# An attention and gated-MLP kernel with a written-out order: 54 steps change places

## The chip, the cores and the metric

The kernel runs on one core of a Trainium2 chip. Times are device microseconds (us) of one launch, from the inputs in HBM to the output in HBM. The time before is 199.52 us, the median of 3 runs (199.38 to 199.70).

Five engines work beside each other: TensorE (PE in the profile, PEld for its weight loads), VectorE (DVE), ScalarE (ACT), GpSimd (POOL) and SyncE (SP), which here only issues transfers. Each engine works through its own list in order. A step that waits holds up everything behind it on its engine.

## The reference

There are two parts. Attention with a sliding window comes first, for 8 batches and 8 heads, 576 positions, 64 values a head; each position sees itself and the 63 before it. The result, 576 x 512 a batch, goes through a gated MLP whose gate mixes positions:

```python
scores = q @ k.T / 8                     # per batch and head
attn   = softmax(where(0 <= i - j < 64, scores, -1e9))
x      = attn @ v                        # heads side by side: 576 x 512
h      = relu(x @ w_in)                  # 512 -> 1024
u, v   = h[:, :512], h[:, 512:]
v_n    = (v - mean(v)) / sqrt(var(v) + 1e-6)
v_s    = w_spatial @ v_n + b_spatial     # 576 x 576, over positions
out    = (u * v_s) @ w_out               # 512 -> 512
```

Inputs and outputs are fp32; the kernel computes products in fp16 with fp32 sums.

## The kernel before

The work is cut into 1,100 or so named steps, and a text, `ORDER`, lists them all. One word is one step: name, engine, and the numbers of the buffers that it takes. `ldq2_0:DQ:0` issues on SyncE the load of q for batch 2, heads 0 to 3, into buffer 0 of its pool; `V1_3:PE:0` runs on TensorE and takes PSUM bank 0. The kernel first makes all steps with what each depends on, and then emits them in the order of the text. So the text alone decides three things: the order on every engine and on the transfer queue, which of the eight PSUM banks a product goes to, and so whose reading of that bank a product has to wait for. Nothing is rescheduled later.

In the names the first number is the batch b (0 to 7). One batch goes through these steps:

- **ldq, ldk, ldv** (DQ): loads. **cq, ck, cv** make fp16 of them, mostly on GpSimd; **tq, tk** (DVE, L416) transpose q and k; **sl, su, s4** make a copy of v that is shifted by 64 positions.
- **S** (PE, L491, L562): scores, into four banks. **E** (ACT, L500, L572): exp. **M** (DVE, L503, L576): the mask, as a minimum. **Z** (PE, L516, L585): sums over keys. **N, n** (ACT, L542, L544): one over the sum, as exp of minus log. **P** (PE, L527, L598): the product with v. **X** (DVE, L535, L606): P times one over the sum, which is x. The suffix r is the last 64 positions.
- **V0 to V4** (PE, L676, L689): the second half of x @ w_in. **Vr** (ACT, L656): relu. **Vb, Va** (DVE, L658, L660): mean and variance. **L1, L2** (ACT, L703, L705): one over the deviation, once a batch, after all five Va. **A** (DVE, L715): v_n, five steps, which all wait for L2. V4 also makes the last 64 rows of the output of the batch before (L692), and so waits for that batch's Ge4.
- **U** (PE, L731, L736) and **Ur** (ACT, L744): the first half, with relu. **G** (PE, L761, L767): w_spatial times v_n, which needs all five A. **Ge** (DVE, L775): times u. **O** (PE, L786): times w_out; it needs Ge0 to Ge3. **Oe** (ACT, L633): to SBUF. **st** (DQ): store.

W and We, cwin, cwsp, cwo are the preparation of the weights, in the first 43 us. Batches overlap: while U and G of batch b run, scores of b + 1 are made, and loads for b + 2 and later are on their way. All loads are issued by SyncE on one queue, in the order of the text.

A product needs its bank to be empty. `G0_1:PE:0` goes into bank 0, which U0_1 had filled, and waits for Ur0_1 on ScalarE to have read it. Where a step of TensorE is moved, its bank is given anew, and so it may wait for another reader than before.

Of the kernel before, what the change touches and what calls it, by code (L numbers as in the profile page):

```python
# [59 lines left out]
Ge1_4:DVE:6 M2_r:DVE cv2_0:POOL:0 cv2_2:POOL sl2_0:POOL:0 su2_2:DVE sl2_2:DVE su2_0:POOL  # L60
cq3_1:POOL:1 cq4_0:POOL:2 ck3_0:POOL:3 N2_00:ACT:4 N2_01:ACT:2 n2_01:ACT s42:ACT n2_00:ACT
Ge1_3:DVE:7 Ge1_0:DVE:8 cq3_0:POOL:0 Z2_r:PE:7 P2_10:PE:5 P2_00:PE:0 Z2_10:PE:4 P2_r:PE:2
P2_01:PE:1 N2_r:ACT:5 n2_r:ACT X2_r:DVE:0 N2_10:ACT:0 n2_10:ACT st0_0:DQ Z2_11:PE:7 N2_11:ACT:3
P2_11:PE:3 V2_4:PE:2 U2_4:PE:4 Vr2_4:ACT:3 n2_11:ACT Oe1_4:ACT:0 X2_00:DVE:0 Ge1_2:DVE:9 X2_01:DVE
X2_10:DVE:1 X2_11:DVE O1_2:PE:0 O1_3:PE:7 Oe1_2:ACT:0 Ur2_4:ACT:4 Oe1_3:ACT tq3_1:DVE:1
tk3_0:DVE:2 V2_2:PE:6 V2_3:PE:1 Vr2_3:ACT:0 tq3_0:DVE:3 S3_1:PE:5:2:3:0 Vr2_2:ACT:2 E3_110:ACT:0
E3_111:ACT V2_0:PE:4 Vr2_0:ACT:6 V2_1:PE:7 Vr2_1:ACT:4 E3_100:ACT:3 S3_0:PE:1:6:3:0 Vb2_3:DVE:3
Va2_3:DVE Vb2_2:DVE:2 M3_11:DVE Vb2_0:DVE:1 ldv3_0:DQ:1 ldv3_1:DQ Va2_2:DVE ldk4_0:DQ:0
ldv3_2:DQ:3 cv3_0:POOL:1 sl3_0:POOL:1 s43:POOL Vb2_4:DVE:4 Va2_4:DVE Va2_0:DVE ck4_0:POOL:1
Vb2_1:DVE:5 Va2_1:DVE E3_000:ACT:2 E3_101:ACT E3_001:ACT M3_00:DVE E3_010:ACT:1 L12:ACT:0 L22:ACT  # L70
st1_1:DQ st0_1:DQ ldv3_3:DQ U2_1:PE:4 U2_0:PE:7 U2_2:PE:5 M3_10:DVE A2_1:DVE:0 ldq4_1:DQ:5
A2_2:DVE:1 ldv4_0:DQ:2 Ur2_0:ACT:3 E3_011:ACT A2_0:DVE:2 Ur2_2:ACT:5 Ur2_1:ACT:1 U2_3:PE:1
O1_0:PE:2 O1_1:PE:6 S3_r:PE:3:7:0:5 Oe1_0:ACT:0 Ur2_3:ACT:2 su3_0:POOL cv3_2:POOL su3_2:POOL
E3_r0:ACT:1 E3_r1:ACT E3_r2:ACT Z3_10:PE:4 Z3_11:PE:2 Z3_00:PE:1 Oe1_1:ACT N3_10:ACT:1 ldv4_1:DQ
sl3_2:POOL cq4_1:POOL:3 ldv4_4:DQ:1 ldk4_1:DQ:4 A2_3:DVE:3 A2_4:DVE ldv4_2:DQ:0 st1_0:DQ
ldq5_0:DQ:6 ldv4_3:DQ st1_4:DQ ldk5_0:DQ:1 E3_r3:ACT N3_11:ACT:5 n3_11:ACT N3_00:ACT:4 cv4_0:ACT:0
G2_3:PE:3 G2_1:PE:7 n3_00:ACT n3_10:ACT M3_01:DVE tq4_0:DVE:4 tk4_0:DVE:5 G2_2:PE:0 G2_0:PE:6
Ge2_3:DVE:0 M3_r:DVE Ge2_1:DVE:1 Z3_r:PE:4 P3_10:PE:5 Z3_01:PE:2 P3_00:PE:1 P3_11:PE:3 N3_r:ACT:2
Ge2_2:DVE:2 P3_01:PE:7 P3_r:PE:0 Ge2_0:DVE:3 N3_01:ACT:0 n3_01:ACT ck4_1:ACT:0 X3_10:DVE:2
X3_00:DVE:3 n3_r:ACT S4_0:PE:4:6:2:5 E4_010:ACT:3 E4_000:ACT:2 X3_01:DVE X3_11:DVE E4_001:ACT  # L80
O2_0:PE:1 Oe2_0:ACT:1 E4_011:ACT G2_4:PE:7 V3_2:PE:3 V3_1:PE:2 ldv5_0:DQ:4 Vr3_2:ACT:5 Vr3_1:ACT:1
V3_0:PE:4 tk4_1:DVE:0 Ge2_4:DVE:4 tq4_1:DVE:1 X3_r:DVE:1 Vr3_0:ACT:7 S4_1:PE:6:7:1:5 ldq5_1:DQ:2
E4_100:ACT:0 E4_110:ACT:1 E4_111:ACT M4_00:DVE M4_01:DVE Z4_00:PE:3 V3_4:PE:0 Vb3_2:DVE:0
# [6 lines left out]
ldv7_4:DQ:0 ldv6_2:DQ:2 Oe2_1:ACT ldv6_3:DQ ldv5_1:DQ ldq6_0:DQ:0 st2_4:DQ Ur3_4:ACT:0 Ur3_2:ACT:2  # L90
Oe2_2:ACT:0 U3_0:PE:3 Oe2_3:ACT n4_01:ACT Ur3_1:ACT:1 cq5_1:POOL:0 su4_0:POOL U3_3:PE:2
Ur3_3:ACT:5 su4_2:POOL G3_2:PE:4 Z4_10:PE:0 Ur3_0:ACT:3 Z4_11:PE:6 Z4_r:PE:5 cq6_1:DVE:3
Ge3_2:DVE:6 sl4_2:POOL P4_10:PE:7 P4_00:PE:1 P4_01:PE:2 N4_10:ACT:4 n4_10:ACT N4_11:ACT:0
N4_r:ACT:5 n4_11:ACT ck5_1:ACT:2 P4_r:PE:3 P4_11:PE:0 X4_00:DVE:0 X4_10:DVE:1 X4_01:DVE G3_0:PE:4
G3_4:PE:1 ldv5_4:DQ:1 S5_0:PE:6:5:7:2 E5_000:ACT:0 E5_001:ACT X4_11:DVE V4_0:PE:0 V4_2:PE:6
# [769 lines left out]
```

## Time and profile before

| what | before |
|---|---|
| median of 3 runs | 199.52 us |
| profiled execution, whole | 199.67 us |
| its span, first to last instruction | 198.0 us |
| TensorE busy | 185.9 us, 94% |
| VectorE busy | 168.7 us, 85% |
| ScalarE busy | 152.3 us, 77% |
| GpSimd busy | 90.8 us, 46% |
| granted TensorE clock | 1.0 |

The page of the profile gives busy time per engine, the span in 40 slices, the chain of work that ended last, and the costliest groups of instructions. The timeline lists instructions by their start in us from the beginning of the span; neighbours of one kind are merged to one row with their count. In square brackets behind a row stands how long the engine had been idle before it, and whose work ended that.

### The profile page before, as it was taken

The numbers are of one execution on the slowest core, as the hardware profiler recorded it, in microseconds if no ns is written. First come the engines' busy times: TensorE is split into PE (matmuls) and PEld (weight loads), VectorE is DVE, ScalarE is ACT, GpSimd is POOL, SyncE is SP. The second block draws the span as 40 slices with busy tenths as digits, with TensorE's granted clock in tenths as the row PEclk, the third lists the DMA queues.
The fourth block names the chain that finished last, engine by engine and source line by source line (L and its number), as shares of the span: only waits on it lengthen the run. The fifth ranks groups of instructions, "written<-read, shape, count | busy, mean of one in ns | idle before, by whom it ended". The sixth has DMA issues, their size and how long they took to land.

```text
span 198.0 us, 7037 instructions
## 1 busy us (share of the span) xinstructions
PE 185.9 (94%) x2953; PEld 99.6 (50%) x2953; DVE 168.7 (85%) x315; ACT 152.3 (77%) x326; POOL 90.8 (46%) x161
## 2 busy tenths in 40 slices
PE   7587999999989999999999999999999999999992
PEld 5464456454435554374546544654456455544450
DVE  5989999998999999999989999987998676538530
ACT  2068699997978989998899797977899986704642
POOL 4077853629668966628937990399200000000000
PEclk9999999999999999999999999999999999999999
DMA  6999999999999999999999969565050000006345
GB/s 208 346 194 360 393 317 244 296 405 280 199 316 318 240 287 259 293 342 367 236 250 256 282 186 304 135 173 193 0 209 10 0 7 3 0 0 220 125 165 209
DMA packets 49506, 42.68 MB, mean 216 GB/s; under 512 B 38593, under 2 KB 38721, under 8 KB 49474
## 3 DMA queue, kind: packets, MB, share of 16 engines
q1 hardware_dynamic: 49250, 41.90, 70.4%
q8 instruction: 23, 0.38, 0.8%
q10 hardware_dynamic: 224, 0.33, 0.5%
q14 instruction: 9, 0.07, 0.1%
HBM read 32.79 MB, written 9.44 MB: 213 GB/s over the span
## 4 chain that ended last, share of the span: by engine, by line
PE 53%; DVE 20%; DMA 13%; SPq 7%; POOL 2%; issue 1%; ACT 0%; POOLq 0%
PE bank L761 12%; PE bank L786 11%; PE bank L731 8%; PE bank L676 7%; DMA nv<-in_v_dram 5%; DMA nk<-in_k_dram 5%; DVE st L658 4%; DMA nq<-in_q_dram 4%; SPq L432 4%; DVE qT L416 4%; DVE vn L715 3%; PE bank L527 3%; DVE e L503 3%; PE bank L491 3%; PE bank L516 2%; DVE kT L416 2%
## 5 line engine op out<-in xcount | busy, mean ns | idle before, releaser
L500 ACT ACTIVATE e<-bank 128x512 f16<-128x512 f32 x64 | 34.6, 602 | 8.9 <-PE bank L491 8.3
L761 PE MATMUL bank<-wspT,vn 128*128 128x512 f16 (+1 forms) x160 | 38.7, 380 | 1.2 <-DVE vn L715 0.9
L775 DVE TENSOR_TENSOR g<-bank,ru 128x512 f16<-128x512 f32 (+1 forms) x40 | 24.5, 625 | 12.2 <-PE bank L761 9.1
L731 PE MATMUL bank<-x,win 128*128 128x512 f16 x128 | 31.1, 379 | 0.0
L656 ACT ACTIVATE vs<-bank 128x512 f16<-128x512 f32 (+1 forms) x40 | 22.7, 601 | 10.5 <-PE bank L676 7.9
L786 PE MATMUL bank<-wout,g 128*128 128x512 f16 x128 | 30.8, 379 | 0.0
L676 PE MATMUL bank<-win,x 128*128 128x512 f16 x128 | 30.7, 379 | 0.0
L633 ACT COPY ob<-bank 128x512 f32<-128x512 f32 (+1 forms) x39 | 22.4, 592 | 9.6 <-PE bank L786 9.3
L306 POOL CAST hq<-nq 128x384 f16<-128x384 f32 x39 | 21.2, 583 | 15.2 <-DMA nq<-in_q_dram 15.2
L306 POOL CAST hv<-nv 128x512 f16<-128x512 f32 x26 | 17.7, 694 | 20.7 <-DMA nv<-in_v_dram 12.3
L658 DVE BATCH_NORM_STATS2 st<-vs 128x6 f32<-128x512 f16 (+1 forms) x40 | 25.6, 665 | 1.5 <-ACT vs L656 1.5
L503 DVE TENSOR_TENSOR e<-e,mask 128x1024 f16<-128x1024 f16 x32 | 25.7, 820 | 0.0
L306 POOL COPY hs<-hv 64x512 f16<-64x512 f16 x36 | 23.8, 685 | 3.1 <-ACT hv L298 1.8
L761 PEld LDWEIGHTS <-vn 128*128 128x128 f16 (+1 forms) x160 | 14.9, 97 | 19.6 <-DVE vn L715 2.5
L744 ACT ACTIVATE ru<-bank 128x512 f32<-128x512 f32 (+1 forms) x40 | 21.6, 570 | 2.9 <-PE bank L736 1.6
L535 DVE TENSOR_TENSOR x<-bank,lz 128x512 f16<-128x512 f32 x32 | 20.4, 676 | 2.6 <-ACT lz L544 2.5
L416 DVE STREAM_TRANSPOSE qT<-hq 128x576 f32<-128x576 f32 x16 | 19.9, 1242 | 1.0 <-POOL hq L306 0.9
L416 DVE STREAM_TRANSPOSE kT<-hk 128x576 f32<-128x576 f32 x16 | 19.8, 1239 | 0.6 <-POOL hk L306 0.6
L544 ACT ACTIVATE lz<-lz 128x512 f32<-128x512 f32 x32 | 20.0, 646 | 0.2
L542 ACT ACTIVATE lz<-bank 128x512 f32<-128x512 f32 x32 | 18.6, 621 | 1.6 <-PE bank L516 1.4
L676 PEld LDWEIGHTS <-x 128*128 128x128 f16 x128 | 11.8, 98 | 14.0 <-issue 0.4
L786 PEld LDWEIGHTS <-g 128*128 128x128 f16 x128 | 11.8, 98 | 13.8 <-DVE g L775 0.8
(85 smaller groups left out, 276.3 us busy)
## 6 DMA issues: line engine op xcount, KB each, us to landing
nq<-in_q_dram SPq DMA_DIRECT2D x16, 576.0 KB, 7.2
nk<-in_k_dram SPq DMA_DIRECT2D x16, 576.0 KB, 7.2
...
```

What stands on the lines that cost most here:

```text
L306: nc.gpsimd.tensor_copy(o[:, lo:lo + step], i[:, lo:lo + step])
L416: d = add(f"t{name}{b}_{g}", ("DVE", 1.09), key, lambda e: nc.vector.transpose(qt.t[:, :].rearrange("p (i j) -> p j i", j=18), h.t[:, :].b ...
L500: ex.append(add(f"E{b}_{g}{u}{w}", ("ACT", 0.475), key, lambda e, u=u, w=w: nc.scalar.activation(e2[u].t[:, w, :], sc[2 * u + w].t[:, :], ...
L503: mins.append(add(f"M{b}_{g}{u}", ("DVE", 0.602), key, lambda e, u=u: nc.vector.tensor_tensor(e2[u].t[:, :, :], e2[u].t[:, :, :], mask[:, ...
L633: lambda e: (nc.vector.tensor_copy if last else nc.scalar.copy)(view(), m.t[rows, 0:n]),
L656: rl = add(f"Vr{b}_{j}", ("ACT", 0.476), key, lambda e: nc.scalar.activation(vs.t[0:jn, :], m.t[0:jn, :], AF.Relu), deps=[pv], acq=[vs], u ...
L658: s1 = add(f"Vb{b}_{j}", ("DVE", 0.595), key + 0.02, lambda e: nc.vector.bn_stats(st6.t[0:jn, 0:6], vs.t[0:jn, :]), deps=[rl], acq=[st6], ...
L676: nc.tensor.matmul(m.t[:, :], xr(b, r)[:, 128 * j:128 * j + 128], w_in_sb[r][:, 512:1024], start=(r == 0), stop=(r == 3))
L731: nc.tensor.matmul(m.t[:, :], w_in_sb[r][:, 128 * i:128 * i + 128], xr(b, r), start=(r == 0), stop=(r == 3))
L761: nc.tensor.matmul(m.t[:, :], w[0:kn, 128 * i:128 * i + 128], wspT[kk][0:kn, 0:512], start=(kk == 0), stop=(kk == 4))
L775: lambda e, m=m, g=g, ru=ru, n=n: nc.vector.tensor_tensor(g.t[:, 0:n], m.t[:, 0:n], ru.t[:, 0:n], ALU.mult),
L786: nc.tensor.matmul(m.t[:, :], G[r][0].t[:, 128 * j:128 * j + 128], w_out_sb[r][:, :], start=(r == 0), stop=(r == 3))
```

## The change

The kernel's functions stay as they are; only `ORDER` differs. No step changes its engine, none is added or removed. Counted on each engine, 18 steps of TensorE, 25 of ScalarE, 9 of VectorE and two transfers stand in another place. On GpSimd the order is the same. Many PSUM banks are numbered anew; most of that is a renaming in which a product still follows the same reader.

The moves, by place (times are those of the profile before):

| place | moves |
|---|---|
| A, 29 to 43 us | cwsp0 ahead of L20; Ur0_2 ahead of N1_00; Ur0_4 behind We4; Ur0_1 ahead of n1_00; W0 ahead of W2; We3 ahead of We2; cwsp4 ahead of A0_1; G0_2 ahead of Z1_r; M1_10 ahead of sl1_1 and su1_1; Z1_10 ahead of P1_r, P1_00, P1_01; N1_10 ahead of cwo10 |
| B, 35 to 57 us | load ldk2_0 ahead of ldq2_0; V1_3 ahead of V1_0 |
| C, 57 to 85 us | G1_4 ahead of Z2_00; Z2_10 ahead of P2_10 and P2_00; M2_r behind sl2_2; Ge1_2 ahead of X2_r; O1_2 ahead of V2_4; n2_11 ahead of Vr2_4; U2_4 from behind V2_4 to behind U2_2, with Ur2_4; V2_3 ahead of V2_2; E3_100 ahead of Vr2_1; U2_0 from behind U2_1 to behind Z3_00, with Ur2_0; store st0_1 ahead of st1_1 |
| D, 85 to 106 us | E4_000 ahead of E4_010; O2_1 ahead of U3_4; Vr3_3 ahead of E4_r0; n4_00 ahead of E4_r1; Ur3_2 and Oe2_1 ahead of L13; L23, Ur3_4 and Oe2_2 ahead of E4_r3; M4_10 ahead of the five A3; tq5_0 ahead of M4_r; P4_00, P4_10, P4_01 ahead of Z4_r; n4_11 ahead of N4_r |
| E, 110 to 113 us | bank of V4_4: after V4_1 (read by Vr4_1) where it was after G3_0 (read by Ge3_0) |
| F, 113 to 121 us | U4_0 from behind Z5_r to ahead of V4_3; U4_4 from behind V4_3 to behind Z5_r, with Ur4_4; N5_00 and E5_111 ahead of Vr4_3; E5_r3 behind Vr4_3; Vb4_3 behind Va4_2, Va4_3 behind M5_r |
| G, 132 to 158 us | Vr5_0 ahead of Vr5_3; Oe4_2 ahead of E6_r3; O4_1 from behind U5_2 to behind G5_4, with Oe4_1 behind n6_01; Z6_00 behind Z6_r; U5_1 ahead of G5_4; n6_00 ahead of n6_01; E7_000 ahead of E7_010; E7_r2 ahead of Vr6_1 |

The core of the diff, for places B, D and F:

```diff
-P1_10:PE:1 X1_r:DVE:1 U1_4:PE:7 M1_11:DVE cwo10:ACT cwo11:POOL N1_10:ACT:3 cwo00:POOL ldq2_0:DQ:0
-ldk2_0:DQ:3 X1_00:DVE:2 Ge0_0:DVE:4 P1_11:PE:3 cwo01:ACT Ur1_4:ACT:5 n1_10:ACT Z1_11:PE:0
...
-ck2_0:POOL:0 tk2_0:DVE:2 cq2_0:POOL:1 O0_2:PE:7 V1_0:PE:6 V1_3:PE:0 ldk2_1:DQ:4 V1_1:PE:2
...
+ldwo0:DQ:0 P1_10:PE:3 X1_r:DVE:1 U1_4:PE:4 M1_11:DVE cwo10:ACT cwo11:POOL cwo00:POOL ldk2_0:DQ:2
+ldq2_0:DQ:3 X1_00:DVE:2 Ge0_0:DVE:4 P1_11:PE:0 cwo01:ACT Ur1_4:ACT:5 n1_10:ACT Z1_11:PE:2
...
+ck2_0:POOL:0 tk2_0:DVE:2 cq2_0:POOL:1 O0_2:PE:4 V1_3:PE:6 V1_0:PE:2 ldk2_1:DQ:4 V1_1:PE:1
...
-ldq6_1:DQ:7 E4_r0:ACT:0 Vr3_3:ACT:2 Vb3_3:DVE:1 Va3_0:DVE E4_r1:ACT E4_r2:ACT n4_00:ACT Va3_3:DVE
-L13:ACT:1 E4_r3:ACT L23:ACT U3_4:PE:0 A3_2:DVE:4 A3_4:DVE A3_0:DVE:5 M4_10:DVE cq5_0:POOL:1
...
+Vr3_3:ACT:2 E4_r0:ACT:0 Vb3_3:DVE:1 Va3_0:DVE n4_00:ACT Ur3_2:ACT:0 E4_r1:ACT E4_r2:ACT Va3_3:DVE
+O2_1:PE:5 Oe2_1:ACT U3_4:PE:6 L13:ACT:1 M4_10:DVE cq5_0:POOL:1 L23:ACT A3_2:DVE:4 A3_4:DVE
...
-Vb4_0:DVE:0 Vb4_1:DVE:4 V4_3:PE:7 Vr4_3:ACT:4 U4_4:PE:2 U4_1:PE:6 N5_00:ACT:2 Va4_4:DVE M5_10:DVE
-Vb4_3:DVE:2 Va4_0:DVE U4_2:PE:4 G3_1:PE:0 ldv5_3:DQ Ur4_4:ACT:4 E5_111:ACT Va4_3:DVE Va4_1:DVE
...
-Z5_01:PE:7 Ur4_1:ACT:2 L14:ACT:0 L24:ACT Z5_r:PE:5 U4_0:PE:2 O3_0:PE:3 Ur4_2:ACT:0 sl6_0:POOL:0
...
+cv6_0:POOL:0 sl5_0:POOL:1 U4_0:PE:1 V4_3:PE:3 Vr4_3:ACT:4 U4_1:PE:0 Vb4_3:DVE:2 U4_2:PE:7
+E5_r3:ACT M5_r:DVE G3_1:PE:4 Va4_3:DVE Ge3_1:DVE:9 Z5_10:PE:5 Z5_01:PE:6 Ur4_1:ACT:4 L14:ACT:0
+L24:ACT Z5_r:PE:3 U4_4:PE:2 Ur4_4:ACT:0 O3_0:PE:0 Ur4_2:ACT:1 sl6_0:POOL:0 cv5_2:POOL A4_2:DVE:0
```

More of the change, by code (lines that the diff above doesn't have):

```diff
@@ new lines @@
+sl1_3:POOL su1_3:POOL N1_r:ACT:2 n1_r:ACT E1_110:ACT:3 E1_111:ACT cv1_1:DVE M1_10:DVE Z1_10:PE:2
+N1_10:ACT:3 sl1_1:DVE ldwo1:DQ:1 su1_1:DVE s41:POOL P1_r:PE:7 Ge0_2:DVE:3 P1_00:PE:5 P1_01:PE:1
+ldwo0:DQ:0 P1_10:PE:3 X1_r:DVE:1 U1_4:PE:4 M1_11:DVE cwo10:ACT cwo11:POOL cwo00:POOL ldk2_0:DQ:2
+ldq2_0:DQ:3 X1_00:DVE:2 Ge0_0:DVE:4 P1_11:PE:0 cwo01:ACT Ur1_4:ACT:5 n1_10:ACT Z1_11:PE:2
+V1_4:PE:7 O0_0:PE:5 X1_01:DVE N1_11:ACT:1 n1_11:ACT X1_10:DVE:3 X1_11:DVE Oe0_4:ACT:0 ldq2_1:DQ:5
+ck2_0:POOL:0 tk2_0:DVE:2 cq2_0:POOL:1 O0_2:PE:4 V1_3:PE:6 V1_0:PE:2 ldk2_1:DQ:4 V1_1:PE:1
@@ L60 @@
[L60 to L83, printed above, removed]
@@ L90 @@
[L90 to L95, printed above, removed]
@@ L120 @@
-E6_r3:ACT s47:POOL Ur5_2:ACT:4 Oe4_2:ACT:1 Oe4_3:ACT Oe4_0:ACT:0 Z6_01:PE:0 Z6_11:PE:4 Z6_00:PE:2
-M6_r:DVE A5_0:DVE:4 P6_r:PE:6 Z6_r:PE:3 Oe4_1:ACT P6_00:PE:5 P6_10:PE:7 ck7_0:POOL:0 cq7_0:POOL:2
-A5_2:DVE:5 A5_3:DVE:6 A5_4:DVE N6_r:ACT:5 N6_11:ACT:1 Z6_10:PE:1 n6_r:ACT N6_10:ACT:2 N6_01:ACT:4
-N6_00:ACT:3 n6_10:ACT n6_01:ACT n6_00:ACT A5_1:DVE:7 G5_4:PE:3 su7_2:POOL tq7_0:DVE:2 U5_1:PE:4
-G5_1:PE:1 U5_3:PE:0 Ge5_4:DVE:5 tk7_0:DVE:3 X6_10:DVE:0 Ur5_1:ACT:2 Ur5_3:ACT:0 n6_11:ACT
-X6_00:DVE:1 X6_r:DVE:0 G5_2:PE:3 Ge5_1:DVE:6 Ge5_2:DVE:7 S7_0:PE:2:7:4:5 P6_01:PE:0 X6_01:DVE
@@ new lines @@
+cv2_0:POOL:0 cv2_2:POOL sl2_0:POOL:0 su2_2:DVE sl2_2:DVE su2_0:POOL cq3_1:POOL:1 cq4_0:POOL:2
+ck3_0:POOL:3 E2_r3:ACT N2_00:ACT:4 M2_r:DVE N2_01:ACT:2 n2_01:ACT s42:ACT n2_00:ACT Ge1_3:DVE:7
+Ge1_0:DVE:8 cq3_0:POOL:0 st0_0:DQ Ge1_2:DVE:9 Z2_r:PE:4 Z2_10:PE:7 N2_r:ACT:5 n2_r:ACT P2_10:PE:6
+P2_00:PE:1 P2_r:PE:5 P2_01:PE:3 X2_r:DVE:0 N2_10:ACT:0 n2_10:ACT Z2_11:PE:4 N2_11:ACT:3 P2_11:PE:0
+n2_11:ACT O1_2:PE:2 V2_4:PE:7 Vr2_4:ACT:3 Oe1_4:ACT:0 X2_00:DVE:0 X2_01:DVE X2_10:DVE:1 X2_11:DVE
+O1_3:PE:5 Oe1_2:ACT:0 Oe1_3:ACT tq3_1:DVE:1 tk3_0:DVE:2 V2_3:PE:1 V2_2:PE:4 Vr2_3:ACT:0
@@ new lines @@
+A2_0:DVE:2 Ur2_2:ACT:3 Ur2_1:ACT:5 U2_3:PE:1 O1_0:PE:6 O1_1:PE:4 S3_r:PE:0:5:7:3 Oe1_0:ACT:1
+Ur2_3:ACT:1 su3_0:POOL cv3_2:POOL su3_2:POOL E3_r0:ACT:1 E3_r1:ACT E3_r2:ACT Z3_10:PE:2 Z3_11:PE:6
+Z3_00:PE:1 Oe1_1:ACT N3_10:ACT:1 ldv4_1:DQ sl3_2:POOL cq4_1:POOL:3 ldv4_4:DQ:1 ldk4_1:DQ:4
+A2_3:DVE:3 A2_4:DVE ldv4_2:DQ:0 st1_0:DQ ldq5_0:DQ:6 U2_0:PE:0 Ur2_0:ACT:2 ldv4_3:DQ st1_4:DQ
+ldk5_0:DQ:1 E3_r3:ACT N3_11:ACT:5 n3_11:ACT N3_00:ACT:4 cv4_0:ACT:0 G2_3:PE:5 G2_1:PE:7 n3_00:ACT
+n3_10:ACT M3_01:DVE tq4_0:DVE:4 tk4_0:DVE:5 G2_2:PE:4 G2_0:PE:2 Ge2_3:DVE:0 M3_r:DVE Ge2_1:DVE:1
@@ new lines @@
+E5_010:ACT:3 E5_011:ACT Vr4_0:ACT:6 tq5_1:DVE:0 Vr4_1:ACT:0 Vr4_2:ACT:3 G3_3:PE:1 tk5_1:DVE:1
+M5_00:DVE Ge3_4:DVE:5 X4_r:DVE:0 Ge3_0:DVE:7 S5_r:PE:4:3:6:2 E5_r0:ACT:1 E5_r1:ACT E5_r2:ACT
+V4_4:PE:7 Z5_00:PE:5 Vr4_4:ACT:5 S5_1:PE:0:4:3:6 tq6_1:DVE:4 Ge3_3:DVE:8 E5_110:ACT:2 E5_100:ACT:1
+Oe3_4:ACT:0 E5_101:ACT M5_01:DVE Vb4_2:DVE:5 Vb4_4:DVE:3 Vb4_0:DVE:0 Vb4_1:DVE:4 N5_00:ACT:2
+Va4_4:DVE M5_10:DVE Va4_0:DVE ldv5_3:DQ E5_111:ACT Va4_1:DVE Va4_2:DVE cv5_0:POOL:1 cq6_0:POOL:1
+cv6_0:POOL:0 sl5_0:POOL:1 U4_0:PE:1 V4_3:PE:3 Vr4_3:ACT:4 U4_1:PE:0 Vb4_3:DVE:2 U4_2:PE:7
@@ new lines @@
+Ur5_2:ACT:0 Oe4_3:ACT Oe4_0:ACT:1 Z6_01:PE:4 Z6_11:PE:6 M6_r:DVE A5_0:DVE:4 P6_r:PE:2 Z6_r:PE:3
+Z6_00:PE:1 P6_00:PE:5 P6_10:PE:0 ck7_0:POOL:0 cq7_0:POOL:2 A5_2:DVE:5 A5_3:DVE:6 A5_4:DVE
+N6_r:ACT:5 N6_11:ACT:1 Z6_10:PE:7 n6_r:ACT N6_10:ACT:2 N6_01:ACT:4 N6_00:ACT:3 n6_10:ACT n6_00:ACT
+n6_01:ACT A5_1:DVE:7 U5_1:PE:3 G5_4:PE:6 O4_1:PE:7 Oe4_1:ACT su7_2:POOL tq7_0:DVE:2 G5_1:PE:4
+U5_3:PE:1 Ge5_4:DVE:5 tk7_0:DVE:3 X6_10:DVE:0 Ur5_1:ACT:4 Ur5_3:ACT:1 n6_11:ACT X6_00:DVE:1
+X6_r:DVE:0 G5_2:PE:6 Ge5_1:DVE:6 Ge5_2:DVE:7 S7_0:PE:0:5:7:2 P6_01:PE:3 X6_01:DVE E7_000:ACT:1
```

152 lines of the change are left out of this document (81 added, 71 removed).

## The prediction

> **What bounds the kernel now.** I read the page first: which engine is full, and what the chain that ended last is made of. Then the list of waits of TensorE alone, from 27 us on, where the preparation is over. Then the table of busy time by stretches, with borders where those waits lie.
>
> ```profile
> span 198.0 us, 7037 instructions
> PE 185.9 (94%) x2953; PEld 99.6 (50%) x2953; DVE 168.7 (85%) x315; ACT 152.3 (77%) x326; POOL 90.8 (46%) x161
> PE 53%; DVE 20%; DMA 13%; SPq 7%; POOL 2%; issue 1%; ACT 0%; POOLq 0%
> ```
>
> ```profile
> PE bank L761 <- DVE vn L715: 0.9, 1, 0.9
> PE bank L585 <- DVE er L576: 0.5, 1, 0.5
> PE bank L491 <- DVE x L535: 0.4, 1, 0.4
> PE bank L736 <- DVE x L606: 0.3, 1, 0.3
> PE bank L689 <- DVE g L775: 0.3, 1, 0.3
> PE bank L761 <- ACT ru L744: 0.2, 1, 0.2
> PE bank L491 <- issue: 0.2, 1, 0.2
> ```
>
> The list (us in total, times, longest) is complete: 2.8 us of idle TensorE in 171. The amount of work is the same after the change, so what can be won is about these 2.8 us, plus some tenths of waits that hide inside a row of matmuls. What can be lost has no such bound.
>
> The next table has for each stretch its length, then busy us of PE, PEld, DVE, ACT and POOL, the granted clock, the share of the DMA engines and GB/s.
>
> ```profile
> 43.20:56.20 13.00, 13.00 (x186) 6.11 (x182) 12.33 (x23) 11.21 (x23) 9.85 (x20) 1.00 1.00 255
> 56.20:58.50 2.30, 1.40 (x8) 0.62 (x8) 2.30 (x4) 2.20 (x5) 1.33 (x3) 1.00 1.01 379
> 58.50:79.50 21.00, 21.00 (x389) 10.88 (x387) 20.83 (x37) 18.25 (x43) 15.71 (x27) 1.00 0.95 280
> 79.50:88.00 8.50, 7.99 (x167) 4.44 (x166) 8.50 (x14) 7.97 (x16) 3.62 (x7) 1.00 1.02 310
> 129.00:198.00 69.00, 65.25 (x795) 32.79 (x793) 45.28 (x91) 46.35 (x100) 10.57 (x19) 1.00 0.27 94
> ```
>
> The chain of work in order of time (start, us) has TensorE's last piece:
>
> ```profile
> 193.69 0.58 PE bank L799 x8
> ```
>
> To 88 us TensorE and VectorE are both nearly full. TensorE's waits at 57 and 80 to 87 us are for VectorE, so VectorE's list is what counts there. The stretch from 129 us is TensorE's alone: the last matmul ends at 194.27, and of the 65.27 us up to there it is busy 65.25. There a reordering can only cost. The clock is 1.00 throughout.
>
> **The change, part by part.**
>
> *A, 29 to 43 us: nothing.* G0_1 no longer stands in the way of its bank: Ur0_1, which reads it, comes two steps of ScalarE earlier (the 0.2 us for L744 in the list goes). But a few steps on, U1_4 waits for X1_r anyway (the 0.3 us for L606), and X1_r stands behind Ge0_2 on VectorE, whose work ahead of it is the same. M1_10 ahead of sl1_1 and su1_1 makes P1_r later by some tenths, which that same wait of U1_4 covers. Without the cover it would cost about 0.3; with a full gain of G0_1 it would bring 0.2.
>
> *B, 35 to 57 us: 0.85 us won.* This is the largest term.
>
> ```profile
> 43.75 1.87 DVE L535 TENSOR_TENSOR x<-bank,lz 128x512 f16<-128x512 f32 x3
> 44.75 1.41 POOL L306 CAST hk<-nk 128x384 f16<-128x384 f32 x3 [2.99 <-DMA nk<-in_k_dram]
> 46.10 2.76 POOL L306 CAST hq<-nq 128x384 f16<-128x384 f32 x6
> 46.19 1.26 DVE L416 STREAM_TRANSPOSE kT<-hk 128x576 f32<-128x576 f32 x1 [0.58 <-POOL hk L306]
> 47.55 1.26 DVE L416 STREAM_TRANSPOSE qT<-hq 128x576 f32<-128x576 f32 x1
> 47.80 1.55 ACT L656 ACTIVATE vs<-bank 128x512 f16<-128x512 f32 x3 [1.14 <-PE bank L676]
> 41.10:44.70 3.60, 3.32 (x71) 2.10 (x65) 3.60 (x7) 3.20 (x7) 0.61 (x1) 1.00 1.03 413
> ```
>
> GpSimd sat 2.99 us until k (ldk2_0, issued second) had landed at about 44.7, cast it, then cast q (ldq2_0, issued first, already there). VectorE had nothing to do from 45.62 to 46.19. With k issued first, GpSimd can start on whichever lands first. In the last row, a stretch as above, the queue moved 413 GB/s; one load of 576 KB takes 1.4 us at that rate, so the first of the two lands near 43.2. Then hk is done at 44.6, ahead of VectorE's 45.62; hq starts at 44.75 when the second has landed, and is done at 46.16. tk2_0 runs from 45.6 to 46.8, tq2_0 to 47.95, against 48.81 before: 0.85 us. Next behind it on VectorE is Vb1_3, which needs Vr1_3; ScalarE waited for V1_3 until 47.80. That is why V1_3 has to go first: a product is 0.87 us (four products in the stretch of 3.4 us), so Vr1_3 ends at 47.55, in time. Without that exchange the gain would stop there. From there to A1_0 VectorE's list has no gap, and G1_2, which waited 0.9 us for A1_0 (the 0.9 for L761 in the list, in the stretch from 56.2), starts 0.85 earlier. TensorE is full from 43.2 to 56.2, so it could not start more than 0.9 earlier. Bounds: 0 if both loads land together, 0.9 if VectorE gains more.
>
> *C, 57 to 85 us: nothing.* Eleven moves, and on TensorE they shift waits about. But in the rows above VectorE is busy 20.83 of 21.00 us and then 8.50 of 8.50. What it does is the same but for the places of M2_r and Ge1_2, each ahead of its first reader: Z2_r comes on TensorE when M2_r is just done, and O1_2, now ahead of V2_4, when Ge1_2 is. VectorE hands the 0.85 us through, to A2_4 (for which G2_3 waits) and to X3_10 (for which S4_0 waits, the 0.4 us). U2_0 goes behind Z3_00 into the gap ahead of G2_3; its 0.87 us are taken out ahead of that gap and put into it, and its bank comes free there with E3_r0. If that fails it costs at most some 0.4 us, and S4_0's wait takes that up. st0_1 ahead of st1_1: the first has its data long before, the second still waits for Oe1_3; nothing behind them on the queue is late.
>
> *D, 85 to 106 us: nothing by itself, 0.4 us for VectorE.*
>
> ```profile
> 98.89 0.30 ACT L703 ACTIVATE ln<-mv,eps_t 128x5 f32<-128x5 f32 x1 [0.30 <-DVE mv L660]
> 99.48 1.05 DVE L715 TENSOR_SCALAR vn<-vs,mv,ln 128x512 f16<-128x512 f16 x3 [0.62 <-ACT ln L705]
> 100.46 0.68 DVE L503 TENSOR_TENSOR e<-e,mask 128x1024 f16<-128x1024 f16 x1
> ```
>
> VectorE sits 0.62 us between the last Va3 and A3_2, until L13 and L23 are through ScalarE. M4_10 (0.68) moves into that hole. Against it, Ur3_2 and Oe2_1 now stand ahead of L13, some 1.0 us of ScalarE. ScalarE had 0.30 spare there, E4_r3 goes behind L23, and Vr3_3 ahead of E4_r0 fills a short wait for S4_r: L23 comes 0.2 to 0.35 later. Net, A3_1 is 0.3 to 0.5 earlier. TensorE gets to G3_2 as before, so this only makes room for E.
>
> *E, 110 to 113 us: 0.5 us won.*
>
> ```profile
> 59.51 0.26 PE bank L562 x32
> 110.87 0.55 PE L562 MATMUL bank<-qT,kT 32*64 32x64 f16 x32
> 111.69 0.38 PE L689 MATMUL bank<-win,x 128*64 128x512 f16 x1 [0.27 <-DVE g L775]
> 110.63 0.41 DVE L606 TENSOR_TENSOR x<-bank,lz_r 128x256 f16<-128x256 f32 x1
> 110.96 0.67 DVE L775 TENSOR_TENSOR g<-bank,ru 128x512 f16<-128x512 f32 x1
> ```
>
> S5_r takes 0.55 us instead of 0.26 because its last bank waits for X4_r (111.04), and V4_4 then 0.27 for Ge3_0 (111.63), which reads its bank. Together 0.56. V4_4's new bank was read by Vr4_1, done earlier, so the 0.27 goes in any case, and Z5_00, one step later, gets the wait for Ge3_0 with 0.9 us to spare. The 0.29 at S5_r goes when VectorE is 0.3 ahead, by D. I take 0.5; bounds 0.27 and 0.56, and below nothing if D goes wrong.
>
> *F, 113 to 121 us: 0.4 us won.*
>
> ```profile
> 114.46 0.63 PE L736 MATMUL bank<-x,win 128*128 128x64 f16 x16
> 114.93 1.89 PE L731 MATMUL bank<-x,win 128*128 128x512 f16 x8
> 118.94 0.30 PE L585 MATMUL bank<-er,ones 128*64 128x128 f16 x4 [0.49 <-DVE er L576]
> 119.17 1.04 PE L731 MATMUL bank<-x,win 128*128 128x512 f16 x4
> 120.05 0.59 PE L786 MATMUL bank<-wout,g 128*128 128x512 f16 x2
> ```
>
> TensorE waits 0.49 us at Z5_r for M5_r. U4_0 (0.88 from start to next start) now lies ahead of the wait and U4_4 (0.47) behind, so 0.41 of work fills the hole. In exchange V4_3 is 0.9 later, and Vr4_3 stands behind N5_00 and E5_111 (but no longer E5_r3) on ScalarE; Vb4_3 is moved back by three Va and M5_r still has Vb4_3 ahead of it. I find M5_r about where it was. Bounds: 0.49 won, 0.3 lost if Vr4_3 comes late.
>
> *G and the rest: nothing.* No wait in TensorE after 129 us can be won. O4_1 goes behind G5_4, into the bank that N6_10 frees; U5_1 and Z6_00 only swap with neighbours. Oe4_1 is later with O4_1, and st4_0 with it, but behind that on the queue come only stores. Vr5_0 ahead of Vr5_3 takes a wait out of VectorE, which has spare time there. Between 0.2 won and 0.5 lost, if O4_1 gets to its bank before N6_10 has read it.
>
> Sum: 0.85 + 0.5 + 0.4 = 1.75 us. The profiled execution took 199.67 us (span 198.0 and 1.67 around it), 0.15 above the median; 199.52 - 1.75 = 197.8.
>
> **The rivals.**
>
> *The pair of loads lands together.* No row shows when the first of them landed. If both end near 44.7, hk is ready as before, B gives nothing, and the time is 199.52 - 0.9 = 198.6.
>
> *Nothing comes of it.* B's gain is given back at a bank in C and E's needs D. Then all that is left is V4_4's bank, under 0.3: 199.3. For it speaks how tight C's exchanges are (Ge1_2, M2_r); against it that VectorE alone sets the pace there.
>
> *Slower: v_n meets GpSimd.* The five A of a batch take 1.8 times as long in one place as in another; the columns are DVE's and POOL's for these instructions alone.
>
> ```profile
> 54.00:57.20 3.20, 0.03 (x1) 0.04 (x2) 3.05 (x5) 0.00 (x0) 1.00 0.94 289
> 119.30:121.20 1.90, 0.00 (x0) 0.00 (x0) 1.69 (x5) 0.00 (x0) 1.00 0.84 276
> 98.95 0.60 POOL L306 CAST hv<-nv 128x512 f16<-128x512 f32 x1
> 102.91 1.44 POOL L306 CAST hv<-nv 128x512 f16<-128x512 f32 x1 [3.35 <-DMA nv<-in_v_dram]
> ```
>
> At 54 to 57 us GpSimd is at work, at 119 it is idle: 0.27 us for each A. GpSimd is paced by landings (here it waits 3.35 us), VectorE after the change is not. If A3 moved into GpSimd's time, and A4 too, VectorE would lose 2 x 1.36 = 2.7 us; TensorE, with 1 us or so of room, would lose 1.1 to 2, against at most 0.9 from B: 200.3. It decides once more than five of these ten are slowed. Against it: A3 starts 0.7 us earlier and only its first step then meets the cast that ends at 99.55.
>
> The Trainium skill, page SBUF — State Buffer, section Who interferes with whom, says that VectorE's tensor_scalar and GpSimd take one port pair in turn, and that the loser waits for the whole of the other's instruction. By that rule an A could lose a whole cast of 0.60 us, ten of them 6.0 us where I have 2.7, and this rival would end at up to 203.6, an estimate. The trace agrees that the two meet, but shows 0.27 us for each A.
>
> **How the numbers follow.** Forecast (B, E, F as summed) 0.59; loads together 0.16; nothing 0.08; slower 0.17. The likeliest gives 197.8, by itself 196.9 to 198.4. The range goes from 196.8, where nearly all of the 2.8 us are won, to 199.7, which leaves out the slower case. A difference under 0.2% (0.4 us) could not be told from none: faster 0.75, same 0.08, slower 0.17.
>
> **What would show it.** B: hk starts near 43.2, and the wait of L761 for vn at 57 us is under 0.2. D: no wait of 0.6 us ahead of A3. E: L562 back at 0.26 and L689 without a wait. F: the 0.49 ahead of L585 mostly gone. Wrong if hk still starts at 44.7, or if new waits of TensorE after 58 us add up to over 1 us.

## The result, and the profile after

The changed kernel takes 198.53 us (median of 23 runs, 196.13 to 204.59), the kernel before 199.72 beside it. The ratio is 0.9912, with an interval of 0.9888 to 0.9936; it leaves out executions that are over 1.5% above the fastest of their kernel, which the medians hold. On the 199.52 us of the prediction that is 1.76 us less, between 1.3 and 2.2; the two medians lie 1.2 us apart. Forecast were 197.8, that is 1.72 us less, in a range of 196.8 to 199.7.

The execution that was profiled first took 204.59 us. The lines here are of a second profile of the same kernel, of an execution of 198.16 us (after_again below). First from its page:

```profile
span 196.3 us, 7029 instructions
PE 186.7 (95%) x2953; PEld 99.9 (51%) x2953; DVE 167.7 (85%) x315; ACT 153.2 (78%) x326; POOL 92.4 (47%) x161
```

Then the list of TensorE's waits from 27 us on (us in total, times, longest), complete:

```profile
PE bank L491 <- issue: 1.2, 1, 1.2
PE bank L491 <- DVE x L535: 0.4, 1, 0.4
PE bank L585 <- DVE er L576: 0.2, 1, 0.2
PE bank L736 <- DVE x L606: 0.2, 1, 0.2
```

Of the waits of before, the 0.9 us for v_n at L761, the 0.3 at L689 and the 0.2 for L744 are gone. The 0.5 at L585 (Z5_r) is gone too: the 0.2 that stands there now is Z2_r at 62 us, waiting for M2_r. The 0.4 for x at S4_0 is as it was. The 0.2 at L491, for which the list has no releaser ("issue"), has become 1.2.

Place B, in order of time (start, us, engine and line, then in brackets the idle time ahead and what ended it), GpSimd first and VectorE below:

```profile
42.55 1.42 POOL L306 CAST hk<-nk 128x384 f16<-128x384 f32 x3 [0.89 <-DMA nk<-in_k_dram]
44.54 1.42 POOL L306 CAST hq<-nq 128x384 f16<-128x384 f32 x3 [0.57 <-DMA nq<-in_q_dram]
```
```profile
43.92 1.27 DVE L535 TENSOR_TENSOR x<-bank,lz 128x512 f16<-128x512 f32 x2
45.12 1.24 DVE L416 STREAM_TRANSPOSE kT<-hk 128x576 f32<-128x576 f32 x1
46.21 1.23 DVE L416 STREAM_TRANSPOSE qT<-hq 128x576 f32<-128x576 f32 x1
47.29 1.81 DVE L658 BATCH_NORM_STATS2 st<-vs 128x6 f32<-128x512 f16 x3
```

k lands near 42.5 and q near 44.5. VectorE has no gap from X1_11 through both transposes into Vb1_3; before, it had 0.58 us ahead of the first transpose.

Places D, E and F:

```profile
97.35 0.78 DVE L503 TENSOR_TENSOR e<-e,mask 128x1024 f16<-128x1024 f16 x1
98.15 1.70 DVE L715 TENSOR_SCALAR vn<-vs,mv,ln 128x512 f16<-128x512 f16 x5
```
```profile
109.32 0.47 PE L562 MATMUL bank<-qT,kT 32*64 32x64 f16 x32
109.72 0.40 PE L689 MATMUL bank<-win,x 128*64 128x512 f16 x1
116.83 0.28 PE L585 MATMUL bank<-er,ones 128*64 128x128 f16 x4
```

The hole of 0.62 us ahead of A3 is filled by M4_10. S5_r (L562) takes 0.47 where it took 0.55, and where 0.26 was foretold; V4_4 (L689) and Z5_r (L585) follow without a wait.

The wait of 1.2 us lies inside S6_0, of whose 64 matmuls 48 run and 16 come later. The first two rows are of the changed kernel, the last two of the kernel before, which stood still at the same matmul, for a shorter time:

```profile
125.09 0.66 PE L491 MATMUL bank<-qT,kT 32*64 32x128 f16 x48
126.97 0.31 PE L491 MATMUL bank<-qT,kT 32*64 32x128 f16 x16 [1.22 <-issue]
```
```profile
127.62 0.66 PE L491 MATMUL bank<-qT,kT 32*64 32x128 f16 x48
128.44 0.31 PE L491 MATMUL bank<-qT,kT 32*64 32x128 f16 x16 [0.16 <-issue]
```

### The profile page after: what moved, and what is told of

It is laid out like the page before. It is cut to its first block, busy times and chain, and to the rows that moved or that the text cites. A ratio compares the mean times of both kernels' runs of the same rounds, so it can differ in the third digit from the quotient of the medians.

```text
span 202.7 us, 7029 instructions
## 1 busy us (share of the span) xinstructions
PE 189.2 (93%) x2953; PEld 100.6 (50%) x2953; DVE 171.7 (85%) x315; ACT 153.4 (76%) x326; POOL 91.8 (45%) x161
## 4 chain that ended last, share of the span: by engine, by line
PE 43%; DVE 33%; DMA 8%; SPq 5%; ACT 5%; issue 3%; POOL 1%; POOLq 0%
PE bank L761 10%; PE bank L786 9%; PE bank L731 7%; PE bank L676 7%; DVE e L503 5%; DVE vn L715 5%; DMA ws<-in_moe_w_spatial_dram 5%; DVE qT L416 5%; DVE kT L416 4%; DVE g L775 4%; DVE x L535 4%; DMA wi<-in_moe_w_in_dram 3%; SPq L432 3%; DVE st L658 3%; PE bank L491 2%
## 5 line engine op out<-in xcount | busy, mean ns | idle before, releaser
L761 PE MATMUL bank<-wspT,vn 128*128 128x512 f16 (+1 forms) x160 | 39.7, 388 | 0.2 <-ACT ob L633 0.2
L731 PE MATMUL bank<-x,win 128*128 128x512 f16 x128 | 31.9, 383 | 0.1
L786 PE MATMUL bank<-wout,g 128*128 128x512 f16 x128 | 31.3, 380 | 0.0
L306 POOL CAST hq<-nq 128x384 f16<-128x384 f32 x39 | 22.1, 607 | 15.5 <-DMA nq<-in_q_dram 15.1
L503 DVE TENSOR_TENSOR e<-e,mask 128x1024 f16<-128x1024 f16 x32 | 28.2, 898 | 0.1
L744 ACT ACTIVATE ru<-bank 128x512 f32<-128x512 f32 (+1 forms) x40 | 21.4, 566 | 7.3 <-PE bank L736 5.7
L306 POOL CAST hv<-nv 128x512 f16<-128x512 f32 x26 | 17.0, 669 | 18.5 <-DMA nv<-in_v_dram 9.7
L761 PEld LDWEIGHTS <-vn 128*128 128x128 f16 (+1 forms) x160 | 15.3, 99 | 19.2 <-issue 1.8
L306 POOL CAST hk<-nk 128x384 f16<-128x384 f32 x33 | 17.4, 565 | 4.3 <-DMA nk<-in_k_dram 4.3
## 6 DMA issues: line engine op xcount, KB each, us to landing
nv<-in_v_dram SPq DMA_DIRECT2D x8, 128.0 KB, 6.5
```

Of the source, the lines that this page charges most:

```text
L306: nc.gpsimd.tensor_copy(o[:, lo:lo + step], i[:, lo:lo + step])
L503: mins.append(add(f"M{b}_{g}{u}", ("DVE", 0.602), key, lambda e, u=u: nc.vector.tensor_tensor(e2[u].t[:, :, :], e2[u].t[:, :, :], mask[:, ...
L731: nc.tensor.matmul(m.t[:, :], w_in_sb[r][:, 128 * i:128 * i + 128], xr(b, r), start=(r == 0), stop=(r == 3))
L761: nc.tensor.matmul(m.t[:, :], w[0:kn, 128 * i:128 * i + 128], wspT[kk][0:kn, 0:512], start=(kk == 0), stop=(kk == 4))
L786: nc.tensor.matmul(m.t[:, :], G[r][0].t[:, 128 * j:128 * j + 128], w_out_sb[r][:, :], start=(r == 0), stop=(r == 3))
```

## The experiments

Each kernel is an edit of the list of words in ORDER; where a bank or a buffer changes hands, the numbers behind it are renamed so that every step keeps its predecessor. Ratios are against the kernel before, run beside each.

**after_again: the changed kernel once more.**

> The changed kernel once more, because the one execution shown of it stretches single instructions (a matmul step S6_0 of 2.9 us, a VectorE product of 3.3 us) that nothing in the change explains. Theory 1 (the prediction's sum): about 197.8; VectorE waits nothing ahead of tk2_0; G1_2's wait for A1_0 under 0.2; no 0.6 us hole ahead of A3; S5_r about 0.3; Z5_r's wait mostly gone. Theory 2 (the early part A costs what B wins): X1_11 on VectorE ends 0.5 to 1.1 later than the 45.6 of before, G1_2 still waits 0.3 or more, and the gain of the whole comes from E and F alone.

Ratio 0.9919 (0.9884 to 0.9953), lines above. The signs of theory 1 are there but one: no wait ahead of tk2_0, none at G1_2, no hole ahead of A3, no wait at Z5_r; S5_r, expected at 0.3, takes 0.47. X1_11 ends at 45.19, not later than before, and theory 2 falls.

**b_only: place B alone.**

```diff
-ldq2_0:DQ:0 ldk2_0:DQ:3
+ldk2_0:DQ:0 ldq2_0:DQ:3
-V1_0:PE:6 V1_3:PE:0
+V1_3:PE:6 V1_0:PE:0
```

> The kernel before with place B alone: ldk2_0 ahead of ldq2_0 on the queue, V1_3 ahead of V1_0 on TensorE. Theory 1: tk2_0 starts with no wait, tq2_0 ends 0.85 us earlier relative to X1_11, G1_2's wait goes from 0.9 to about 0.1, and the 0.85 reaches S4_0: some 198.7, ratio 0.996. Rival 'loads land together': the wait stays 0.58, ratio 1.000. Rival 'given back in C': wait gone, but ratio 1.000 and S4_0's or G2_3's wait grows by the same amount.

Ratio 0.9949 (0.9913 to 0.9985): 1.0 us, between 0.3 and 1.7. VectorE has no gap from X1_11 to Vb1_3. Both rivals fall. The rest of the change is worth the difference to 0.9912, some 0.7 us, if it is anything: the intervals overlap.

**a_no_b: the changed kernel without B.**

```diff
-ldk2_0:DQ:2 ldq2_0:DQ:3
+ldq2_0:DQ:2 ldk2_0:DQ:3
-V1_3:PE:6 V1_0:PE:2
+V1_0:PE:6 V1_3:PE:2
```

> The changed kernel with place B undone (ldq2_0 first again, V1_0 ahead of V1_3). Theory 1: 0.85 us slower than the changed kernel, that is about 198.65, ratio 0.9955; the 0.58 us hole ahead of tk2_0 is back. Theory 2 and 'loads together': as fast as the changed kernel, ratio about 0.991.

Ratio 0.9983 (0.9941 to 1.0025). All other places together cannot be told from nothing; B taken away costs 1.3 to 1.4 us, more than the 0.85 foretold. The rows of GpSimd and VectorE (lines of this kernel are four lower):

```profile
45.34 1.41 POOL L302 CAST hk<-nk 128x384 f16<-128x384 f32 x3 [2.92 <-DMA nk<-in_k_dram]
46.79 1.26 DVE L412 STREAM_TRANSPOSE kT<-hk 128x576 f32<-128x576 f32 x1 [1.65 <-POOL hk L302]
```

Here k landed at 45.3 and VectorE waited 1.65 us, not 0.58; in a_only, with the loads in the same order, it waited 0.83, and in ef_only not at all. The hole that B closes is not of one size.

**a_only: the kernel before with place A alone** (the order of the changed kernel up to the loads of batch 2, with these as before).

> The kernel before with place A alone (all moves up to the loads of batch 2, none behind). Theory 1 (A is nothing): ratio 1.000, within 0.002; X1_11 ends at 45.6 as before. Theory 2 (A loses): X1_11 ends 0.5 to 1.1 later and the ratio is 1.002 to 1.004. A third way, a gain of A (Ur0_1 earlier frees G0_1's bank): 0.2 us, ratio 0.999.

Ratio 1.0013 (0.9970 to 1.0056); X1_11 ends at 45.36. A is nothing, within what these runs tell.

**loads_only: the loads exchanged, the products not.**

```diff
-ldq2_0:DQ:0 ldk2_0:DQ:3
+ldk2_0:DQ:0 ldq2_0:DQ:3
```

> The kernel before with the two loads exchanged alone, V1_0 still ahead of V1_3. Prediction's step: Vr1_3 comes one product (0.87 us) later and holds Vb1_3, so that most of the gain stops there: Vb1_3 starts 0.5 us or more after tq2_0's end, ratio 0.998 to 1.000. Rival: the exchange of the products is not needed, ratio 0.995 as b_only.

Ratio 1.0035 (0.9990 to 1.0080): no gain. On VectorE:

```profile
46.41 1.23 DVE L416 STREAM_TRANSPOSE qT<-hq 128x576 f32<-128x576 f32 x1
48.20 2.46 DVE L658 BATCH_NORM_STATS2 st<-vs 128x6 f32<-128x512 f16 x4 [0.56 <-ACT vs L656]
```

The hole has moved behind the transposes, where VectorE now waits 0.56 us for Vr1_3. The exchange of V1_3 and V1_0 is what lets the earlier load count.

**ef_only: the kernel before with places E and F alone** (the order of the changed kernel from P4 to O3_2).

> The kernel before with places E and F alone (the order from P4 to O3_2), without A to D and G. Prediction's terms: V4_4's 0.27 goes, Z5_r's 0.49 mostly goes, S5_r's wait stays since VectorE is not ahead: 0.6 to 0.7 us, ratio 0.9967. If E needs D, only F's 0.4 is left: 0.998. If the hole inside S6_0 swallows it: 1.000 with a hole there larger by 0.6.

Ratio 1.0008 (0.9976 to 1.0039). The expected 0.6 us is outside the interval. In its profile S5_r, V4_4 and Z5_r wait for nothing and S6_0 has no hole, but a wait stands between them, in TensorE's list between 103 and 135 us:

```profile
PE bank L689 <- DVE x L606: 0.5, 1, 0.5
```

This is V5_4, which waits for X5_r. On VectorE ahead of X5_r, M5_01 took 1.41 us (0.66 in a_only) and the five A4 2.32 (1.70 in a_only), both beside a busy GpSimd.

**no_ef: the changed kernel with E and F undone** (from P4 to O3_2 the order of before).

> The changed kernel with places E and F undone (from P4 to O3_2 the order of before). Theory of the prediction (E 0.5 and F 0.4 us): about 198.7, ratio 0.9964. Theory 'E and F only soften a hold of VectorE' (a_only and ef_only): where M5_00 takes 0.7 us the old order waits under 0.3 us at S5_r, V4_4 and Z5_r together, where it takes 1.4 to 2.0 us some 1.0 us; in the median about 0.3 us slower than the changed kernel, ratio 0.992 to 0.994.

Ratio 0.9923 (0.9891 to 0.9955): within 0.1 to 0.2 us of the changed kernel, each known to some 0.5 to 0.6 us. The waits came back:

```profile
PE bank L491 <- issue: 1.1, 1, 1.1
PE bank L585 <- DVE er L576: 0.5, 1, 0.5
PE bank L689 <- DVE g L775: 0.3, 1, 0.3
```

This is TensorE's list between 103 and 135 us. So E and F take real waits away, and the time does not show it.

**before_again: the kernel before once more.**

> The kernel before once more, for a second profile of it. If the long M5_00 on VectorE (0.67 to 3.51 us in the six profiles so far, other M steps 0.68) and the hole inside S6_0 on TensorE (0.4 to 2.2 us lost) come by chance from execution to execution, both sizes differ here from the 1.43 and 0.36 of the first profile; if they belong to the order of the steps, they are again 1.4 and 0.4. Ratio 1.000.

One execution, of 204.21 us (span 202.5). M5_00 took 3.53 us and the hole in S6_0 was 1.07, where the first profile of the same order had 1.43 and 0.40: both sizes come from execution to execution, and neither belongs to the order of the steps.

M5_00 is the minimum of one E of batch 5 and the mask; behind it on VectorE stand Ge3_4, X4_r and Ge3_0, for which S5_r and V4_4 wait. Here it is in after_again, with GpSimd at the same time:

```profile
107.02 1.73 DVE L503 TENSOR_TENSOR e<-e,mask 128x1024 f16<-128x1024 f16 x1
```
```profile
105.92 1.17 POOL L306 COPY hs<-hv 64x512 f16<-64x512 f16 x2
107.04 1.17 POOL L306 CAST hv<-nv 128x512 f16<-128x512 f32 x2
108.16 1.06 POOL L306 CAST hs<-nv 64x512 f16<-64x512 f32 x1
```

and in a_only (lines three lower):

```profile
109.26 0.67 DVE L500 TENSOR_TENSOR e<-e,mask 128x1024 f16<-128x1024 f16 x1
```
```profile
109.29 1.67 POOL L303 CAST hv<-nv 128x512 f16<-128x512 f32 x2
```

In the one, GpSimd's two casts of hv pass at full speed (1.17 us for two), and VectorE gets its turn with the cast behind them (1.06 us where 0.61 is usual). In the other VectorE went first, and it is GpSimd's two casts that took 1.67 us.

**pool_gap: a gap on GpSimd.**

```diff
-cv6_0:POOL:0 sl5_0:POOL:1 ... sl6_0:POOL:0 cv5_2:POOL ... s45:POOL ... ldk6_0:DQ:5 ... ck6_0:POOL:0
+cv6_0:POOL:0 ldk6_0:DQ:5 ck6_0:POOL:0 sl5_0:POOL:1 ... sl6_0:POOL:0 cv5_2:POOL ... s45:POOL
```

> The changed kernel with GpSimd's ck6_0 moved ahead of sl5_0, sl6_0, cv5_2 and s45 (its load stays in its place of the queue), so that GpSimd waits for a landing just when VectorE starts M5_00. Theory 'GpSimd without a gap holds VectorE off': M5_00 takes 0.7 to 1.1 us, S5_r waits for nothing, and the time is 0.2 to 1.0 us below the changed kernel, ratio 0.987 to 0.991. Rival 'something else lengthens M5_00': it takes 1.4 to 3.5 us as before, ratio 0.992.

Ratio 0.9900 (0.9862 to 0.9939), not to be told from the changed kernel. M5_00 takes 0.67 and S5_r waits for nothing:

```profile
107.21 0.67 DVE L503 TENSOR_TENSOR e<-e,mask 128x1024 f16<-128x1024 f16 x1
```
```profile
107.03 1.89 POOL L306 CAST hv<-nv 128x512 f16<-128x512 f32 x2
110.10 2.13 POOL L306 CAST hk<-nk 128x384 f16<-128x384 f32 x3 [1.18 <-DMA nk<-in_k_dram]
```

But the gap of 1.18 us opens only at 108.9, when M5_00 is over; VectorE got in during the cast ahead of it (1.89 for 1.17). So the outcome fits the theory and is no proof of it. GpSimd's work moved on into A4, whose five steps took 2.79 us in place of 1.70, and V5_4 then waited 0.8 us: what was won came back as a loss there.

**s6_late: S6_0 behind two long steps.**

```diff
-S6_0:PE:1:2:7:5 U4_3:PE:0 G4_1:PE:6
+U4_3:PE:0 G4_1:PE:6 S6_0:PE:1:2:7:5
```

> The changed kernel with S6_0 behind U4_3 and G4_1 on TensorE. Theory 'instruction fetch': the hole inside S6_0 ends 2.5 us after a 16 KB packet of the instruction queue that starts while the short matmuls of P5 run; with 2.1 us of long matmuls put in between, TensorE's wait with no releaser (1.2 us in after_again) goes under 0.2 us, and the time falls by about 1.0 us against the changed kernel: ratio about 0.987. Rival 'S6_0 itself' (its operands or banks): the hole moves along with S6_0, ratio 0.992 as the changed kernel.

Ratio 0.9907 (0.9878 to 0.9936). TensorE's list between 103 and 135 us is empty: the hole is gone and did not move along with S6_0. The full 1.0 us is not in the time; the interval reaches down to 0.9878, so a part of it may be.

Where the hole opens can be counted. It stands at the same place, ahead of the 49th matmul of S6_0 (the 2143rd of the kernel), in each of the eight profiles that have one, the one of the kernel before among them. In the table it goes from the start of TensorE's last instruction ahead of it, weight loads included, to the start of the next. The packets of the instruction queue (q8 on the page) have their own times in the trace:

```
kernel         packet starts   hole from   to       packet's start to hole's end, us
after_again    124.47          125.51      126.97   2.49
a_only         125.99          127.25      128.35   2.36
no_ef          126.31          127.38      128.67   2.36
a_no_b         127.57          128.07      129.86   2.29
b_only         129.00          129.94      131.38   2.38
before_again   130.73          132.08      133.15   2.43
after          129.26          129.30      131.51   2.25
before         126.17          128.03      128.43   2.27
```

The page of after_again has the queue's sum (packets, MB, share of the DMA engines):

```profile
q8 instruction: 23, 0.38, 0.9%
```

23 packets for TensorE's 5,906 weight loads and matmuls are one for every 257. S6_0 alone has 128 and takes 0.76 us without a hole, and the short matmuls of P5 run just ahead. This fits TensorE coming to the end of the instructions that it has before the next packet serves it; what it has in hand, no row shows. In ef_only, loads_only and pool_gap, which have no hole with S6_0 in its old place, the packet starts 2.3 to 2.7 us ahead of the 49th matmul; in after_again it starts 1.0 us ahead of the hole. Why it starts earlier in some executions stays open.

**late_two: s6_late with M5_00 behind Ge3_0.**

```diff
-M5_00:DVE Ge3_4:DVE:5 X4_r:DVE:0 Ge3_0:DVE:7
+Ge3_4:DVE:5 X4_r:DVE:0 Ge3_0:DVE:7 M5_00:DVE
```

> The changed kernel with two more moves: M5_00 on VectorE behind Ge3_0, so that a hold of it by GpSimd no longer delays X4_r and Ge3_0, and S6_0 behind U4_3 and G4_1 as in s6_late. If S5_r's waits come from the hold of M5_00: S5_r takes 0.33 us and V4_4 waits for nothing even where M5_00 takes 1.4 us or more, Z5_00 takes up to 0.6 us without a wait; no wait with no releaser at S6_0; about 0.5 to 1.0 us below the changed kernel, ratio 0.987 to 0.990. If VectorE is late for another reason there, S5_r's wait for X4_r stays and the ratio is 0.991 as s6_late.

Ratio 0.9895 (0.9850 to 0.9939). M5_00 took 0.99 us and S5_r 0.33, V4_4 waited for nothing. The foretold case, a long M5_00 without a wait behind it, did not come about here; b_two has it. It is the lowest ratio of all, and with this interval it can't be told from the changed kernel.

**b_two: the kernel before with B and the two late moves, nothing else.**

> The kernel before with place B and the two late moves of late_two (M5_00 behind Ge3_0, S6_0 behind U4_3 and G4_1), and nothing of A and C to G. If B carries the change, and the stalls at M5_00 and S6_0 the rest: S5_r takes 0.33 us, no wait with no releaser at S6_0, ratio 0.989 to 0.992, as the changed kernel or a little below it. If the many small moves of C to G carry something, it stays at b_only's 0.995.

Ratio 0.9967 (0.9925 to 1.0008). The traits came (M5_00 took 1.93 us, S5_r 0.33, no hole in S6_0), the time did not: it is nearer to b_only's 0.9949 than to the changed kernel's. The two late moves bring nothing that these runs can show, and something in the rest of the change may.

## Why the prediction was right, point by point

The sum of 1.75 us and the measured 1.76 agree better than their terms do, and with an interval of 1.3 to 2.2 that they agree so closely is luck. The table has, from all profiles, the us between the ends of named steps, and the length of M5_00; those with a star are of executions above 200 us, and the means below go by the others.

```
                 X1_11's end   X1_11 to G1_2   G1_2 to S5_0   S5_0 to G4_3   G4_3 to O7_4   M5_00
before             45.62         12.81           48.74          26.04          61.03        1.43
a_only             45.36         13.03           49.10          25.64          60.85        0.67
ef_only            45.34         12.47           49.81          25.44          60.86        0.67
loads_only         45.39         12.64           48.67          26.00          60.99        1.73
b_two              45.02         11.60           49.56          26.06          60.85        1.93
no_ef              45.40         11.55           49.51          26.98          60.85        1.46
after_again        45.19         11.76           48.65          26.13          60.85        1.73
s6_late            46.42         11.81           48.72          25.51          60.86        1.83
pool_gap           44.98         11.57           48.88          26.33          60.86        0.67
late_two           45.32         11.73           49.14          25.04          61.40        0.99
before_again *     45.70         14.43           48.30          29.50          60.85        3.53
b_only *           45.34         11.80           49.06          29.95          60.85        3.51
a_no_b *           45.13         13.70           48.99          26.82          60.86        2.00
after *            46.71         12.08           49.01          30.14          61.08        3.31
```

*A, nothing:* right. X1_11 ends at 45.45 in the mean of the six profiles with A's order, at 45.34 in the four without, and a_only's ratio is 1.0013.

*B, 0.85:* right in its mechanism, down to the step that Vr1_3 would stop it (0.56 us in loads_only), and somewhat small. One reason given is not right: GpSimd's list has the cast of k ahead of that of q in both kernels, so it can't start on whichever lands first; what the exchange does is to have k land first. In the second column the six profiles with the whole of B have 11.67 in the mean, the three without any of it (before, a_only, ef_only) 12.77: 1.1 us, over the bound of 0.9 that the prediction took from one execution's wait at G1_2 (1.12 in a_only). b_only's 1.0 us agrees, and a_no_b's 1.3 to 1.4 do within their intervals. The prediction took k's landing at 44.7 from one execution. With q first, GpSimd's cast of k begins between 43.4 and 44.8 in these three, and at 45.3 and 46.9 in the two with a star; with k first, in nine profiles, between 42.0 and 43.6. The rival "loads land together" is out: in after_again q landed 2 us behind k.

*C, nothing, and D, nothing by itself:* right as far as can be seen. In the third column the old order has 49.18 in the mean of five profiles, the new 48.98, and each scatters by about 1 us. The one sign against C is Z2_r's new wait of 0.2 us: M2_r is not "just done" when Z2_r comes, but a little late. S4_0's wait for VectorE stands behind it and took it up.

*E, 0.5, and F, 0.4:* here the prediction failed. The waits at V4_4 and Z5_r went as it said. S5_r's did so in part: it takes 0.47 us, and its time without a wait is 0.33 (a_only, ef_only, pool_gap), not the 0.26 that the prediction took from the chain, so that at most 0.49 could be won by E. S6_0 starts 19.48 us behind S5_0 in after_again, and 20.45 to 20.78 in before, no_ef and loads_only; but ef_only has 20.21, and a_only, without E and F, 19.34. To the end of G4_3, just behind S6_0, no_ef needs 26.98 us and after_again, which differs from it by E and F alone, 26.13: in this pair, both with a hole in S6_0, nearly the whole 0.9 is there. In before and loads_only, with a short hole or none, the old order needs no more than after_again, 26.04 and 26.00; and with M5_00 at 0.67 old and new need 25.64 and 25.44 (a_only, ef_only). The times give less than 0.9: 1.0008 for E and F alone, at most 0.5 us won; 0.9923 against 0.9912 and 0.9919 without them.

Three things lie behind it that the prediction did not see. The first: the waits at S5_r and V4_4 hung on M5_00's 1.43 us. a_only, with 0.67, has neither of them in the old order, nor the one at Z5_r; and in b_two, where M5_00 takes 1.93 but stands behind Ge3_0, S5_r takes its 0.33. The second: where M5_00 is not held, a later step of VectorE can be, as in ef_only, and then V5_4 waits. The third: the 0.2 for L491 with no releaser, the last line of the prediction's list, was put at nothing, without a reason, by "No wait in TensorE after 129 us can be won". It is the hole in S6_0, at 128.0 to 128.4, which was short in that execution. In eight of the eleven profiles with S6_0 in its old place it is there, with 0.4 to 2.2 us, and whatever is won ahead of it meets it. That this hole takes E's and F's gain each time is not shown, since no_ef has one too. The prediction's own sign of being wrong, new waits of TensorE after 58 us of over 1 us, came true with the 1.2 us at L491 (0.2 before) and the 0.2 of Z2_r; the time came out right all the same, in part because B paid more.

*G, nothing:* right; the fifth column has 60.85 to 61.03 in the old order and 60.85 or 60.86 in the new, late_two (61.40) apart.

*The slower rival:* A3 and A4 took 1.7 us each in both profiles of the changed kernel, as beside an idle GpSimd. In no_ef and pool_gap, with the same order around A3, it took 2.27 and 2.99, and A4 took 2.79 in pool_gap and 2.32 in ef_only, so the meeting does come about in some executions, at 0.6 to 1.3 us. The same mechanism sits at M5_00, in the kernel before already: there it ends at 110.37, with one step between it and the X4_r whose row the prediction quoted. The prediction does not have it. No run took GpSimd's work away; that GpSimd holds M5_00 off rests on the rows of both engines.

The Trainium skill, page SBUF — State Buffer, section Who interferes with whom, says that a tensor_tensor with both inputs in SBUF meets GpSimd's reads, and calls the lock on the shared ports exclusive: whoever has it keeps it for the whole instruction, and the other is blocked. The trace agrees in so far as the casts that VectorE waits for run at their full speed. But in after_again VectorE was held for 1.06 us (1.73 less 0.67), through two casts of GpSimd, not one.

What stays open: between b_only's 0.9949 and the changed kernel's 0.9912 lie 0.7 us. The table has 0.2 for C and D, within the scatter. For E and F it has 0.85 from one pair of profiles, 1.0 from another (b_two 26.06, late_two 25.04, neither with a hole, but these differ in the other places too), and 0.2 or nothing from the rest. b_two, with B and without those places, stays at 0.9967. The medians of all runs, on the other hand, put b_only at 198.50 us, level with the changed kernel's 198.53 and 198.17. Whether the rest of the change is worth anything or this is chance is not settled.
